# First pair of an attention kernel: other load buffers, its own shift chain for head a's first 12 maxima, and pair 1's preparations inside the first block

## The chip, the cores and the metric

The kernel runs on one core of one Trainium2 chip. The metric is device time in microseconds of one execution. The engines are TensorE (PE, matmuls, with the weight loads counted apart as PEld), VectorE (DVE), ScalarE (ACT), GpSimd (POOL) and SyncE (SP), whose queue issues most DMAs.

## What is computed

Attention over 2 batches of 8 heads, whose queries are pooled two by two, followed by two feed-forward layers:

```python
q_pool = q.reshape(B, H, S // 2, 2, D).mean(axis=3)          # B=2 H=8 S=1152 D=64
scores = np.matmul(q_pool, k.transpose(0, 1, 3, 2)) / np.sqrt(D)
scores = scores - np.max(scores, axis=-1, keepdims=True)
attn = np.exp(scores)
attn = attn / (np.sum(attn, axis=-1, keepdims=True) + 1e-09)
x = np.matmul(attn, v)                                       # to 1152 tokens x 512
h = x @ w_in                                                 # d_ff 2048
g = (a[0] + a[1]*h + a[2]*h*h + a[3]*h*h*h) / (1 + abs(b[0])*abs(h) + abs(b[1])*h*h + 1e-6)
x = g @ w_out
h = x @ w2_in
out = (np.maximum(h, 0) + np.log1p(np.exp(-np.abs(h)))) @ w2_out
```

## The kernel before

All matmuls work on numbers split into a high and a low part of 32 bits, so each product is made from two or three matmuls. The attention runs over eight pairs of heads (a and b of a pair; `j` is the pair, `x` the head), the feed-forward layers follow.

For each pair the kernel first *prepares*: it loads K and Q, adds the queries two by two (`prep_q`, L317 and L318 on POOL), transposes K and Q on PE (`tr_k` L328, `tr_q` L353), casts the high part out of PSUM on ACT (L334, L361), subtracts the low part on DVE (L123 is the subtraction helper, L362), and copies the results by DMA to where each head needs them: `dma_ks` (K's two parts, `KS`), `dma_q` (`QQ`, `QL`), `dma_kh` (a second place of K's high part, `KH`). The buffers `kr`, `qr`, `qs`, `khi`, `klo`, `qhi`, `qlo` and `vr` exist once each. V is split by `prep_v` (L310 on ACT, then a subtraction; for head a on POOL, for head b on DVE).

Then come the *maxima*: 27 fills (`p1_fill`, L397) put 128 pooled queries against 384 keys each into PSUM, and `p1_max` (L402, DVE) takes the largest score of each row. Fill `u` belongs to tile `u // 3`: tiles 0 to 3 are head a, tile 4 is half a and half b and takes four matmuls instead of two, tiles 5 to 8 are head b. The *shift chain* turns the maxima into ten further rows of the query operand: `shift_a` (three small DVE operations, L410, L411, L123), `shift_t` (a matmul, L419), `shift_m` (two DVE products, L426 and L433, into rows 64 to 73 of `QL`). A head's chain waits for 15 maxima.

Then comes the *block* of 36 steps (`s_step`, two matmuls L447 and L448, exponential L451 on ACT). Steps 0 to 17 are head a, in two halves of the queries, steps 18 to 35 head b. Every two steps `s_split` casts the probabilities (L458, ACT) and subtracts (L123, POOL), and `pv` multiplies by V (L470 to L472). PSUM has three tiles `s` (scores, transpositions, shift), three `p1` (maxima) and two for the sums.

The order is written by hand as due times: `A(t, f)` puts function f at step t, where block j starts at step 36 j. `b0`, `b1`, `b2` are the starts of blocks j, j-1 and j-2. A pair is prepared from `b2` on and its maxima are made from `b1` on, so in the steady state pair j+1's maxima and pair j+2's preparations run inside block j. A planner then sorts each engine's queue: what its own model has ready and is due first goes first; within a queue nothing overtakes. `behind(f, ...)` queues f behind the last recorded instruction of the engines named.

The first pair is special. `first_load` (L228) loads K and Q of head a on SP's queue and of head b on ACT's, into `kr` and `qr`. `first_k` and `first_q` transpose each head by itself, with no DMA between. PE runs 24 dummy matmuls at the start (`warm`, L265) and one behind each fill of the first pair. Pair 1's preparations are due beside the first pair's maxima, before block 0 (`k1`, lines "o = b2 + ..."). `constants` and `moe_consts` are queued behind the first pair's splits. Clears and constants stand at the end of the function (L732 to L740).

Of the kernel before, what the change touches and what calls it, by code (L numbers as in the profile page):

```python
# [19 lines left out]
    wu=1,  # L20
# [51 lines left out]
    k1=1,  # L72
# [15 lines left out]
def attn_moe_kernel(tc, q, k, v, w1_in, w1_out, moe_a, moe_b, w2_in, w2_out, out):  # L88
# [140 lines left out]
    def first_load():  # L229
        kr = early.tile([128, C, 2, D], F32, tag="kr", name="kr").rearrange("p c x d -> p (c x d)")  # L230
        kr = kr.rearrange("p (x c d) -> p x c d", x=2, d=D)
        qr = early.tile([128, 2, 5, 2, D], F32, tag="qr", name="qr")
        qs = early.tile([128, 5, 2, D], F32, tag="qs", name="qs")
        for x, eng in enumerate((nc.sync, nc.scalar)):
            eng.dma_start(out=kr[:, x].rearrange("p c d -> p (c d)"),
                          in_=k[0, x].rearrange("(p c) d -> p (c d)", p=128))
            eng.dma_start(
                out=qr[:, x, 0:4].rearrange("p t r d -> p t (r d)"),
                in_=q[0, x, 0:1024].rearrange("(t p r) d -> p t (r d)", p=128, r=2),
            )  # L240
            eng.dma_start(out=qr[0:64, x, 4].rearrange("p r d -> p (r d)"),
                          in_=q[0, x, 1024:S].rearrange("(p r) d -> p (r d)", r=2))
        st["kr", 0], st["qr", 0], st["qs", 0] = kr, qr, qs

    def constants():
        nc.vector.tensor_copy(out=identr, in_=ident)
        nc.vector.tensor_add(out=mask, in0=ident[0:10, 0:5], in1=ident[0:10, 5:10])
        nc.vector.memset(eps, 1e-9)
        for x in range(2):
            nc.gpsimd.memset(KH[x][64:74].bitcast(F32), 1.0)  # L250
# [16 lines left out]
    def first_k(x, g):  # L267
        kr = st["kr", 0]
        t = pps.tile([128, 512], F32, tag="s", name="tk")[0:64, 0:384]
        for i in range(3):  # L270
            nc.tensor.transpose(t[:, i * 128:(i + 1) * 128], kr[:, x, 3 * g + i], ident)
# [103 lines left out]
    def p1_fill(j, u):  # L375
# [4 lines left out]
        if j == 0 and u % 2:  # L380
# [19 lines left out]
    def p1_max(j, u):  # L400
        t, e = divmod(u, 3)
        nc.vector.tensor_reduce(out=st["nm", j][:, t, e:e + 1], in_=st.pop(("p1", j, u)), axis=AX.X,  # L402
                                op=ALU.max, negate=True)

    def shift_a(j, x):
        c = slice(0, 5) if x == 0 else slice(4, 9)
# [3 lines left out]
        nc.vector.tensor_reduce(out=m, in_=nm, axis=AX.X, op=ALU.min)  # L410
# [11 lines left out]
    def shift_m(j, x):  # L422
# [3 lines left out]
        nc.vector.tensor_tensor(  # L426
            out=ql[64:74, c0:c0 + 512].rearrange("p (t i) -> p t i", t=4),
            in0=t[0:10, 0:128].unsqueeze(1).to_broadcast([10, 4, 128]),
            in1=mask[:, m0:m0 + 4].unsqueeze(2).to_broadcast([10, 4, 128]),
            op=ALU.mult,  # L430
        )
        m1, c1, i1 = (4, 512, 0) if x == 0 else (0, 64, 64)
        nc.vector.tensor_scalar(out=ql[64:74, c1:c1 + 64], in0=t[0:10, i1:i1 + 64],  # L433
                                scalar1=mask[:, m1:m1 + 1], scalar2=None, op0=ALU.mult)
# [66 lines left out]
    for j in range(NP):  # L501
# [407 lines left out]
```

## Time and profile before

| | us |
|---|---|
| median of 3 runs (lowest, highest) | 762.19 (761.78, 762.73) |
| the profiled execution | 762.84 |
| its span, first to last instruction | 761.0 |

| engine | busy us | share of the span |
|---|---|---|
| PE | 727.4 | 96% |
| PEld | 680.8 | 89% |
| DVE | 552.6 | 73% |
| ACT | 493.7 | 65% |
| POOL | 294.0 | 39% |

The shares are means over stages with different limits. A matmul's end is modelled, so PE's busy time is no measure of how densely matmuls follow one another; their starts are. "Idle before" in a row is the time in which the engine stood still ahead of that instruction, with what ended it.

### The profile page before, as it was taken

How to read it: one execution, taken by the hardware profiler on the slowest of the kernel's cores; microseconds unless marked ns; L12 is line 12 of the kernel's file. 1: busy time of each engine (PE TensorE's matmuls, PEld its weight loads, DVE VectorE, ACT ScalarE, POOL GpSimd, SP SyncE). 2: the span in 40 equal slices, each digit the busy share in tenths (PEclk: the TensorE clock that was granted, in tenths of full speed). 3: DMA queues.
4: the chain of work that ended last, by engine and by line, in shares of the span. 5: the costliest groups of instructions: out<-in, count | busy, mean ns of one | idle time of the engine just before them, and what ended most of it. 6: DMA issues, size and time to landing. Idle time of an engine off the chain costs nothing.

```text
span 761.0 us, 11752 instructions
## 1 busy us (share of the span) xinstructions
PE 727.4 (96%) x4273; PEld 680.8 (89%) x4273; DVE 552.6 (73%) x885; ACT 493.7 (65%) x921; POOL 294.0 (39%) x233
## 2 busy tenths in 40 slices
PE   8999999999999998888999999999999899999997
PEld 5699999999999997668999999999889779989986
DVE  5777767787777679999999999999987772111122
ACT  3278888888888888986778777866744552222120
POOL 5278796969697877760000000000133432000000
PEclk9999999999999999999999999999999999999999
DMA  4866365646453434332211122221234440001011
GB/s 130 204 154 156 93 159 123 141 114 151 117 114 85 99 99 124 112 115 79 82 58 56 56 84 60 79 70 45 87 105 139 139 139 0 1 1 42 0 42 42
DMA packets 60473, 70.30 MB, mean 92 GB/s; under 512 B 20008, under 2 KB 48512, under 8 KB 60416
## 3 DMA queue, kind: packets, MB, share of 16 engines
q1 hardware_dynamic: 59232, 68.58, 33.4%
q10 hardware_dynamic: 1184, 0.98, 0.4%
q8 instruction: 33, 0.54, 0.3%
q14 instruction: 24, 0.20, 0.1%
HBM read 47.71 MB, written 2.36 MB: 66 GB/s over the span
## 4 chain that ended last, share of the span: by engine, by line
PE 68%; DVE 15%; ACT 8%; issue 3%; DMA 3%; POOL 1%; DVEq 0%; ACTq 0%; POOLq 0%; SPq 0%
PE h L610 18%; PE p L397 10%; PE acc L702 10%; PE acc L660 9%; PE pv L472 4%; PE s L448 4%; PE s L447 4%; PE pv L470 4%; PE pv L471 4%; DMA wraw<-in_moe_w_in_dram 3%; DVE pk L189 3%; DVE pk L183 2%; ACT p L451 2%; ACT ph L458 2%; DVE gl L123 1%
## 5 line engine op out<-in xcount | busy, mean ns | idle before, releaser
L123 POOL TENSOR_TENSOR pl<-p,ph 128x576 fp32r<-128x576 f32 x144 | 209.7, 1471 | 60.9 <-ACT ph L458 40.9
L610 PE MATMUL h<-xh,w 128*128 128x384 f32 x768 | 198.7, 338 | 5.9 <-DVE p L635 5.9
L402 DVE TENSOR_REDUCE nm<-p 128x1 f32<-128x384 f32 x216 | 116.6, 552 | 44.8 <-PE p L397 43.2
L610 PEld LDWEIGHTS h<-xh,w 128*128 128x128 f32 x768 | 140.5, 190 | 8.7 <-issue 6.7
L123 POOL TENSOR_TENSOR w<-pk,w 128x512 fp32r<-128x512 f32 x26 | 39.4, 1517 | 252.4 <-PE h L610 187.6
L451 ACT ACTIVATE p<-s 128x288 f32<-128x288 f32 x288 | 114.5, 408 | 28.2 <-PE s L448 26.8
L610 PE MATMUL h<-xl,w 128*128 128x384 f32 x384 | 129.9, 338 | 0.0
L123 DVE TENSOR_TENSOR gl<-p,gh 128x768 fp32r<-128x768 f32 (+1 forms) x49 | 48.3, 989 | 100.4 <-ACT gh L621 100.3
L472 PE MATMUL pv<-pl,v 128*128 128x288 f32 x288 | 88.3, 307 | 10.8 <-POOL pl L123 10.7
L458 ACT CAST ph<-p 128x576 fp32r<-128x576 f32 x144 | 96.8, 672 | 2.7
L660 PE MATMUL acc<-gh,w 128*128 128x384 f32 x384 | 91.8, 336 | 1.5 <-ACT gh L621 1.5
L702 PE MATMUL acc<-w,gh 128*128 128x512 f32 x288 | 90.3, 394 | 2.2 <-ACT gh L621 1.6
L470 PE MATMUL pv<-ph,v 128*128 128x288 f32 x288 | 86.5, 301 | 0.4 <-ACT ph L458 0.4
L471 PE MATMUL pv<-ph,v 128*64 128x288 f32 x288 | 85.3, 296 | 0.0
L690 ACT ACTIVATE p<-h 128x768 f32<-128x768 f32 (+1 forms) x25 | 19.5, 783 | 90.0 <-PE h L610 90.0
L610 PEld LDWEIGHTS h<-xl,w 128*128 128x128 f32 x384 | 72.8, 190 | 0.0
L660 PEld LDWEIGHTS acc<-gh,w 128*128 128x128 f32 x384 | 68.6, 188 | 2.6 <-ACT gh L621 2.4
L472 PEld LDWEIGHTS pv<-pl,v 128*128 128x128 f32 x288 | 54.6, 190 | 17.9 <-POOL pl L123 17.6
L702 PEld LDWEIGHTS acc<-w,gh 128*128 128x128 f32 x288 | 53.4, 188 | 13.9 <-ACT gh L621 2.4
L189 DVE SCALAR_TENSOR_TENSOR pk<-wraw,pk 128x512 int32<-128x512 int32 x64 | 58.5, 917 | 1.0
L660 PE MATMUL acc<-gl,w 128*128 128x384 f32 x192 | 58.3, 337 | 0.9 <-DVE gl L123 0.9
L702 PE MATMUL acc<-w,gl 128*128 128x512 f32 x144 | 57.1, 396 | 1.5 <-DVE gl L123 1.5
(147 smaller groups left out, 1479.0 us busy)
## 6 DMA issues: line engine op xcount, KB each, us to landing
wraw<-in_moe_w_in_dram SPq DMA_DIRECT2D x32, 512.0 KB, 4.5
wraw<-in_moe_w_out_dram SPq DMA_DIRECT2D x32, 512.0 KB, 3.2
vr<-in_v_dram SPq DMA_DIRECT2D x8, 576.0 KB, 3.7
kr<-in_k_dram SPq DMA_DIRECT2D x15, 288.0 KB, 3.9
qr<-in_q_dram SPq DMA_DIRECT2D x15, 256.0 KB, 3.4
out_dram<-m SPq DMA_DIRECT2D x15, 128.0 KB, 1.7
kha<-ks0a SPq DMA_DIRECT2D x4, 288.0 KB, 3.0
khb<-ks0b SPq DMA_DIRECT2D x4, 288.0 KB, 4.7
```

What stands on the lines that cost most here:

```text
L123: return eng.tensor_tensor(out=o, in0=a, in1=b, op=ALU.subtract)
L189: nc.vector.scalar_tensor_tensor(out=g, in0=raw[:, :, 0], scalar=29, in1=g, op0=ALU.logical_shift_right, op1=ALU.bitwise_or)
L397: m = nc.tensor.matmul(out=o, lhsT=l, rhs=r, start=(a == 0), stop=(a == len(mm) - 1))
L402: nc.vector.tensor_reduce(out=st["nm", j][:, t, e:e + 1], in_=st.pop(("p1", j, u)), axis=AX.X, op=ALU.max, negate=True)
L451: st["last", "exp"] = nc.scalar.activation(out=st["p"][:, s % 2], in_=t, func=AF.Exp).ins
L458: nc.scalar.copy(out=ph, in_=p)
L470: nc.tensor.matmul(out=st["pv", j, g], lhsT=h, rhs=ph, start=(c == 0), stop=False)
L471: nc.tensor.matmul(out=st["pv", j, g][0:64], lhsT=l, rhs=ph, start=False, stop=False)
L472: nc.tensor.matmul(out=st["pv", j, g], lhsT=h, rhs=pl, start=False, stop=(c == C - 1))
L610: nc.tensor.matmul(out=h, lhsT=w[:, wi, wd], rhs=x[:, d, xcols(c)], start=(n == 0), stop=(n == 3 * ND - 1))
L660: nc.tensor.matmul(out=st["acc", c, d], lhsT=w[:, wi, wd], rhs=g, start=(first and n == 0), stop=(last and n == 2))
L702: nc.tensor.matmul(out=st["acc", c, t], lhsT=g[:, t * 128:(t + 1) * 128], rhs=w[:, wi], start=(first and n == 0), stop=(last and n == 2))
```

## The change

It changes only the opening and blocks 0 and 1.

- `first_load` brings K of both heads on SP's queue and Q of both on ACT's, into buffers of the probabilities (tags `p`, `pl`, and `xs0` for the last 64 rows of Q), which leaves `kr` and `qr` to pair 1.
- Constants and clears go to the start of the program; six clears move from POOL to DVE: four of 10 x 640, and two of 10 x 1152 that were part of `constants`. `moe_consts` goes to step 39.
- For the first pair, fills 0 to 11 are followed by a chain of head a's first four tiles (`part=1`), at high priority. Fills 12 to 14 come after it. Fills 15 to 26, the other twelve of head b, are due in steps 0 to 11 of block 0, without dummies behind them. The rest of head a's shift (`part=2`, 64 columns) is due at step 3, head b's chain at step 14.
- Pair 1's preparations move into block 0: query sums due at step -14, key transpositions at 2, 5 and 8, query transpositions at 11 and 14, copies at 11 (K of a), 15 (Q of a), 16 (K of b), 17 (Q of b). Its 27 fills are due one a step from 18 to 44, its chains from 34 and 46. Pair 2's due times stay: loads at 0, query sums at 8, key transpositions at 12, 15 and 18.
- The first pair's second V subtraction goes from DVE to POOL.

```diff
-    k1=1,
+    k1=26,
+    p1s=18,
...
+        rest = late.tile([128, HALF], F32, tag="xs0", name="qrest")[0:64, 0:256]
+        rest = rest.rearrange("p (x r d) -> p x r d", x=2, r=2)
+        kr, qr = [], []
+        for x in range(2):
+            kx = late.tile([128, 2, HALF], F32, tag="p", name="kr0", bufs=4).rearrange("p a b -> p (a b)")
+            qx = late.tile([128, 2, HALF], F32, tag="pl", name="qr0", bufs=5).rearrange("p a b -> p (a b)")[:, 0:512]
+            nc.sync.dma_start(out=kx, in_=k[0, x].rearrange("(p c) d -> p (c d)", p=128))
+            nc.scalar.dma_start(
+                out=qx.rearrange("p (t e) -> p t e", t=4),
                 in_=q[0, x, 0:1024].rearrange("(t p r) d -> p t (r d)", p=128, r=2),
             )
+            nc.scalar.dma_start(out=rest[:, x].rearrange("p r d -> p (r d)"),
+                                in_=q[0, x, 1024:S].rearrange("(p r) d -> p (r d)", r=2))
...
-        (nc.gpsimd if T["qsp"] and x else nc.vector).tensor_add(out=qs[p, c, x], in0=qr[p, x, c, 0], in1=qr[p, x, c, 1])
+        a = qr[x] if g == 0 else st["rest"][:, x].unsqueeze(1)
+        nc.vector.tensor_add(out=qs[p, c, x], in0=a[:, :, 0], in1=a[:, :, 1])
...
-        sub(nc.gpsimd if T["vl"] > x else nc.vector, v2[:, :, 128:192], vr, v2[:, :, 0:64])
+        sub(nc.gpsimd if T["vl"] > x or j == 0 else nc.vector, v2[:, :, 128:192], vr, v2[:, :, 0:64])
...
-        if j == 0 and u % 2:
+        if j == 0 and u < 15 and u % 2:
...
+    def shift_a(j, x, part=0):
+        n = 4 if part == 1 else 5
+        c = slice(0, n) if x == 0 else slice(4, 9)
...
+        if part == 1:
+            nc.vector.memset(m[:, 4:5], 0.0)
+        nc.vector.tensor_reduce(out=m[:, 0:n], in_=nm, axis=AX.X, op=ALU.min)
...
+    def chain(j, x, part):
+        with tc.high_priority():
+            shift_a(j, x, part)
+            shift_t(j, x)
+            shift_m(j, x, part)
...
-                    A(b1 + T["pv"] + T["pvd"] * x, lambda x=x: behind(lambda: prep_v(1, x), "act", "dves"), pr=7)
+                    A(b1 + T["pv"] + T["pvd"] * x, lambda x=x: behind(lambda: prep_v(1, x), "exp", "max"), pr=7)
...
-            A(b1 + T["ft"] + 1, lambda: behind(constants, "dve"))
-            A(b1 + T["ft"] + 1, lambda: behind(moe_consts, "act", "dve"))
+            A(ST + 3, lambda: behind(moe_consts, "sp", "exp", "max"), pr=9)
...
-            A(o + T["pq"], prep_q, j)
+            A((o if j > 1 else b2 + 14) + T["pq"], prep_q, j)
...
-            A(o + T["ks0"], dma_ks, j, 0)
-            A(o + T["q0"], dma_q, j, 0)
-            A(o + T["ks1"], dma_ks, j, 1)
-            A(o + T["q1"], dma_q, j, 1)
+            for x, (tk, tq) in enumerate(((T["ks0"], T["q0"]), (T["ks1"], T["q1"])) if j > 1 else ((21, 25), (26, 27))):
+                A(o + tk, dma_ks, j, x)
+                A(o + tq, dma_q, j, x)
...
-                t0 = b1 + T["p1o"] + u * 4 // 3
+                t0 = -38 + u if u < 12 else -36 + u if u < 15 else u - 15
                 A(t0, p1_fill, j, u, pr=5)
-                A(t0, lambda: behind(lambda: warm(T["wu"]), "pe"), pr=5)
+                if u < 15:
+                    A(t0, lambda: behind(lambda: warm(T["wu"]), "pe"), pr=5)
                 A(t0 + 1, p1_max, j, u, pr=6)
+            A(-25, chain, 0, 0, 1)
+            A(3, chain, 0, 0, 2, pr=7)
+            A(14, chain, 0, 1, 0, pr=7)
         for u in range(27 if j else 0):
-            t0 = b1 + T["p1o"] + u * 4 // 3
+            t0 = b1 + (T["p1o"] + u * 4 // 3 if j > 1 else T["p1s"] + u)
...
-        for x in range(2):
-            t0 = b1 + T["s0"] if x == 0 else b1 + T["s1"]
+        for x in range(2 if j else 0):
+            t0 = b1 + ((T["s0"], T["s1"]) if j > 1 else (T["p1s"] + 16, T["p1s"] + 28))[x]
...
+        nc.vector.memset(zero, 0.0)
         make_identity(nc, ident)
-        nc.vector.memset(zero, 0.0)
...
-                nc.gpsimd.memset(QL[i][x][64:74].bitcast(F32), 0.0)
+                nc.vector.memset(QL[i][x][64:74].bitcast(F32), 0.0)
+        nc.vector.tensor_copy(out=identr, in_=ident)
+        nc.vector.tensor_add(out=mask, in0=ident[0:10, 0:5], in1=ident[0:10, 5:10])
+        nc.vector.memset(eps, 1e-9)
+        for x in range(2):
+            nc.vector.memset(KH[x][64:74].bitcast(F32), 1.0)
```

## Rows read from the trace of the kernel before

**Rows 1.** The page, its first line.
```profile
span 761.0 us, 11752 instructions
```

**Rows 2.** Busy time by stretch: stretch, length, busy us (instructions) of PE, PEld, DVE, ACT, POOL, granted clock, DMA share, GB/s.
```profile
9.18:34.13 24.95, 23.36 (x120) 15.01 (x118) 21.46 (x51) 6.00 (x14) 7.45 (x10) 1.00 0.62 143
34.13:70.92 36.79, 36.57 (x242) 34.80 (x243) 26.35 (x58) 30.17 (x68) 27.80 (x23) 1.00 0.68 159
70.92:107.60 36.68, 36.68 (x258) 36.19 (x257) 27.28 (x56) 31.45 (x72) 30.04 (x25) 1.00 0.53 124
```

**Rows 3.** Timeline of PE, two stretches: start us, duration us, what.
```profile
70.92 0.30 PE L448 MATMUL s<-ql1a,kha 74*128 74x288 f32 x1
71.06 0.34 PE L397 MATMUL p<-ks0a,qq0a 128*128 128x384 f32 x1
71.23 0.34 PE L397 MATMUL p<-ks0a,ql0a 74*128 74x384 f32 x1
71.41 0.29 PE L470 MATMUL pv<-ph,v 128*128 128x288 f32 x1
...
107.60 0.30 PE L448 MATMUL s<-ql0a,kha 74*128 74x288 f32 x1
```

**Rows 4.** Chain of waits: start us, duration us, what.
```profile
45.94 0.33 PE tk L328 x3
```

**Rows 5.** Timeline of all engines, the first 10 us.
```profile
0.97 0.11 DVE L738 MEMSET qq0a<- 128x64 f32 x1
...
1.06 5.33 PE L265 MATMUL wm<-zero 128*64 128x256 bf16 x24 [1.06 <-DVE zero L732]
...
1.48 0.11 DVE L739 MEMSET ql1b<- 64x64 f32 x1
...
4.48 0.62 POOL L740 MEMSET ql0b<- 10x640 f32 x1
...
5.64 0.43 DVE L279 TENSOR_TENSOR qs<-qr 128x256 f32<-128x256 f32 x1 [4.04 <-DMA qr<-in_q_dram]
...
9.08 1.05 POOL L250 MEMSET kha<- 10x1152 f32 x1
```

**Rows 6.** Timeline of DVE, first maxima and constants.
```profile
9.84 0.56 DVE L402 TENSOR_REDUCE nm<-p 128x1 f32<-128x384 f32 x1 [0.25 <-PE p L397]
...
17.63 0.23 DVE L246 CAST identr<-ident 128x128 fp32r<-128x128 f32 x1
...
17.86 1.40 DVE L256 TENSOR_SCALAR a_sb<-a_sb 128x4 f32<-128x4 f32 x1
...
19.71 2.86 DVE L402 TENSOR_REDUCE nm<-p 128x1 f32<-128x384 f32 x6
```

**Rows 7.** Timeline: shift chains of pairs 0 and 2, first shifted scores.
```profile
32.45 0.23 PE L419 MATMUL ts<-identr,s 128*10 128x128 f32 x1
...
33.40 0.68 DVE L426 TENSOR_TENSOR ql0a<-ts,mask 10x512 fp32r<-10x512 f32 x1
...
34.13 0.40 PE L448 MATMUL s<-ql0a,kha 74*128 74x288 f32 x1
...
35.82 0.17 DVE L410 TENSOR_REDUCE m<-nm 128x5 f32<-128x15 f32 x1
...
90.24 1.42 POOL L123 TENSOR_TENSOR pl<-p,ph 128x576 fp32r<-128x576 f32 x1 [0.67 <-ACT ph L458]
90.25 1.44 DVE L123 TENSOR_TENSOR s<-m,s 128x5 fp32r<-128x5 f32 x1
```

**Rows 8.** Groups by line and form, ACT, 34.13 to 70.79 us.
```profile
L334 ACT CAST khi<-tk 128x384 fp32r<-128x384 f32 x3 | 1.4, 471 | 0.1
```

**Rows 9.** Timeline of POOL: the first pair's first probabilities.
```profile
36.65 4.20 POOL L123 TENSOR_TENSOR pl<-p,ph 128x576 fp32r<-128x576 f32 x3 [4.41 <-ACT ph L458]
```

**Rows 10.** Timeline of SP's queue; landing times of the copies into `ks1b`.
```profile
31.14 1.10 SPq L211 DMA_DIRECT2D qq1a<-qhi  x2
...
DMA to landing us min/median/max: 5.9/5.9/5.9
```

More of the change, by code (lines that the diff above doesn't have):

```diff
@@ L229, in first_load @@
     def first_load():
[L230 to L238, printed above, removed]
+        rest = late.tile([128, HALF], F32, tag="xs0", name="qrest")[0:64, 0:256]
[7 more added lines that the diff above has]
+                out=qx.rearrange("p (t e) -> p t e", t=4),
                 in_=q[0, x, 0:1024].rearrange("(t p r) d -> p t (r d)", p=128, r=2),
             )
[L241 to L248, printed above, removed]
-        for x in range(2):
-            nc.gpsimd.memset(KH[x][64:74].bitcast(F32), 1.0)
+            nc.scalar.dma_start(out=rest[:, x].rearrange("p r d -> p (r d)"),
+                                in_=q[0, x, 1024:S].rearrange("(p r) d -> p (r d)", r=2))
+            kr.append(kx.rearrange("p (c d) -> p c d", d=D))
+            qr.append(qx.rearrange("p (t r d) -> p t r d", t=4, r=2))
+        st["qs", 0] = early.tile([128, 5, 2, D], F32, tag="qs", name="qs")
+        st["kr", 0], st["qr", 0], st["rest"] = kr, qr, rest
     def moe_consts():
@@ L401, in p1_max @@
         t, e = divmod(u, 3)
[L402 to L406, printed above, removed]
+        st["last", "max"] = nc.vector.tensor_reduce(
+            out=st["nm", j][:, t, e:e + 1], in_=st.pop(("p1", j, u)), axis=AX.X, op=ALU.max, negate=True).ins
+    def shift_a(j, x, part=0):
+        n = 4 if part == 1 else 5
+        c = slice(0, n) if x == 0 else slice(4, 9)
         nm = st["nm", j][:, c]
@@ L420, in shift_t, with shift_m @@
         st["ts"] = t
-    def shift_m(j, x):
+    def shift_m(j, x, part=0):
         t = st.pop("ts")
@@ L425, in shift_m @@
         m0, c0 = (0, 0) if x == 0 else (1, 128)
[L426 to L431, printed above, removed]
-        m1, c1, i1 = (4, 512, 0) if x == 0 else (0, 64, 64)
-        nc.vector.tensor_scalar(out=ql[64:74, c1:c1 + 64], in0=t[0:10, i1:i1 + 64],
-                                scalar1=mask[:, m1:m1 + 1], scalar2=None, op0=ALU.mult)
+        if part != 2:
+            nc.vector.tensor_tensor(
+                out=ql[64:74, c0:c0 + 512].rearrange("p (t i) -> p t i", t=4),
+                in0=t[0:10, 0:128].unsqueeze(1).to_broadcast([10, 4, 128]),
+                in1=mask[:, m0:m0 + 4].unsqueeze(2).to_broadcast([10, 4, 128]),
+                op=ALU.mult,
+            )
+        m1, c1, i1 = (4, 512, 0) if x == 0 else (0, 64, 64)
+        if part != 1:
+            nc.vector.tensor_scalar(out=ql[64:74, c1:c1 + 64], in0=t[0:10, i1:i1 + 64],
+                                    scalar1=mask[:, m1:m1 + 1], scalar2=None, op0=ALU.mult)
+    def chain(j, x, part):
[3 more added lines that the diff above has]
+            shift_m(j, x, part)
     def qcols(x, half):
@@ L542, in attn_moe_kernel @@
             for u in range(27):
-                t0 = b1 + T["p1o"] + u * 4 // 3
+                t0 = -38 + u if u < 12 else -36 + u if u < 15 else u - 15
                 A(t0, p1_fill, j, u, pr=5)
-                A(t0, lambda: behind(lambda: warm(T["wu"]), "pe"), pr=5)
+                if u < 15:
+                    A(t0, lambda: behind(lambda: warm(T["wu"]), "pe"), pr=5)
                 A(t0 + 1, p1_max, j, u, pr=6)
+            A(-25, chain, 0, 0, 1)
+            A(3, chain, 0, 0, 2, pr=7)
+            A(14, chain, 0, 1, 0, pr=7)
         for u in range(27 if j else 0):
-            t0 = b1 + T["p1o"] + u * 4 // 3
+            t0 = b1 + (T["p1o"] + u * 4 // 3 if j > 1 else T["p1s"] + u)
             A(t0, p1_fill, j, u, pr=T["prf"])
             A(t0 + T["p1m"], p1_max, j, u, pr=T["prm"])
-        for x in range(2):
-            t0 = b1 + T["s0"] if x == 0 else b1 + T["s1"]
+        for x in range(2 if j else 0):
+            t0 = b1 + ((T["s0"], T["s1"]) if j > 1 else (T["p1s"] + 16, T["p1s"] + 28))[x]
+            d = (8, 8) if j > 1 else (1, 4)
             A(t0, shift_a, j, x)
-            A(t0 + T[f"st{x}"], shift_t, j, x, pr=1)
-            A(t0 + T[f"st{x}"] + T["sm"], shift_m, j, x, pr=2)
+            A(t0 + d[x], shift_t, j, x, pr=1)
+            A(t0 + d[x] + T["sm"], shift_m, j, x, pr=2)
         for s in range(ST):
@@ L730, in attn_moe_kernel @@
     if True:
+        nc.vector.memset(zero, 0.0)
         make_identity(nc, ident)
-        nc.vector.memset(zero, 0.0)
         for i in range(2):
             nc.gpsimd.memset(V2[i][:, :, :, 64:128].bitcast(F32), -1.0)
-        for x in range(2):
-            z = slice(576, 640) if x == 0 else slice(0, 64)
-            for i in range(2):
+        for i in range(2):
+            for x in range(2):
+                z = slice(576, 640) if x == 0 else slice(0, 64)
                 nc.vector.memset(QQ[i][x][:, z].bitcast(F32), 0.0)
                 nc.vector.memset(QL[i][x][0:64, z].bitcast(F32), 0.0)
-                nc.gpsimd.memset(QL[i][x][64:74].bitcast(F32), 0.0)
+                nc.vector.memset(QL[i][x][64:74].bitcast(F32), 0.0)
+        nc.vector.tensor_copy(out=identr, in_=ident)
+        nc.vector.tensor_add(out=mask, in0=ident[0:10, 0:5], in1=ident[0:10, 5:10])
+        nc.vector.memset(eps, 1e-9)
+        for x in range(2):
+            nc.vector.memset(KH[x][64:74].bitcast(F32), 1.0)
         ev.sort(key=lambda e: e[:3])
```

3 lines of the change are left out of this document (1 added, 2 removed).

## The prediction

> **What bounds the kernel now.** I read the span and its stretches first. The span is 761.0 us in an execution of 762.84 us; 1.84 us lie around it, and the median of the runs, 762.19 us, is 0.65 us below that execution [rows 1]. I then cut the attention's start by its own marks: 9.18 us (first matmul of the maxima) to 34.13 (first scores that use a shift), and from there two blocks of 36 steps [rows 2]. The reader should see that the blocks are full: 36.68 us for the second block, TensorE (PE) busy in all of it, its matmuls at a pitch that leaves nothing between them. The opening is not full. Its 60 matmuls of 384 columns are worth 60 x 0.175 = 10.5 us at the pitch of the blocks [rows 3], and its transpositions and the shift about 4 us more (some nine groups like that of [rows 4], and single ones); 24.95 us pass. About 10 us of PE time are lost there, although the busy column says 23.36: it counts matmuls whose ends are modelled, and the dummies. VectorE (DVE) is busy for 21.46 of the 24.95 us, so the opening is bound by DVE: 27 maxima, the splits of the first pair, the constants. That is the only stretch in which this change can gain.
>
> **The start.** Loading the first pair into other buffers brings K on SP's queue and Q on ACT's side by side, and frees the old buffers for pair 1, whose loads no longer wait. The borrowed buffers cost nothing: the transpositions have read them before there are probabilities. The change of queues gains nothing by itself: PE runs its 24 dummies from 1.06 to 6.39 us, and DVE adds the queries from 5.64 on, so data that land earlier find DVE occupied. What occupies it is the other half of the edit. DVE is free at about 1.57 us (eight clears of 64 columns start 0.073 us apart) [rows 5]. To it come four clears of 640 columns and two of 1152, 4864 columns. GpSimd (POOL) needs 4 x 0.62 + 2 x 1.05 = 4.58 us for them, which is one bound; 76 times 0.073 = 5.5 us is the other. I take 5.0, and 0.4 us for the three constants now ahead (the first of them 0.23 [rows 6]). DVE then begins with the queries at 1.57 + 5.0 + 0.4 = 7.0 us rather than 5.64, 1.3 us late. Not all of it reaches the first maximum (9.84 us): in these 4.2 us DVE waits for transpositions that PE can now do meanwhile. I take **+0.8 us**, bounds 0 and 1.8.
>
> **The twelfth maximum.** The six maxima from 19.71 us take 2.86 us, 0.477 each; the twelfth is the fifth of these and ends at 22.1 us. The constants and the expert parameters sat in one stretch ahead, 17.63 to 19.26 us, and leave it: -1.6 us. The splits of head b stay where they are, ahead of most of the maxima. So the twelfth ends at 22.1 - 1.6 + 0.8 = 21.3 us.
>
> **The shift chain.** Now only these twelve are waited for, and the chain goes ahead of other DVE work. Three small operations of 0.17 us, then a matmul of 0.23, then a product of 0.68 [rows 7]; with some 0.1 us for each of five hand-overs 1.9 us. Against it stands a row: a subtraction of five columns took 1.44 us when POOL's 1.42 us subtraction had started just before it [rows 7]. In the new order POOL holds, at 18 to 23 us, both subtractions of V for the first pair (the second came from DVE) and the sums of queries for pair 1, right where the chain falls. The Trainium skill (SBUF — State Buffer, Who interferes with whom) says that a DVE instruction with two SBUF inputs contends with a GpSimd instruction that reads SBUF, and this row agrees; one hold of 1.42 us by that rule gives 759.1 us in all, no contention 757.7. I take +1.1 us for the hold, bounds 0 and 2.8 (two holds). Chain: 3.0 us. First shifted scores at 21.3 + 3.0 = 24.3 us, against 34.13: **-9.8 us**.
>
> **What moves behind it.** PE's work isn't removed. Twelve fills of head b (two matmuls of 0.175 us each) go into block 0: 4.2 us. Pair 1's five groups of transpositions go there too: 5 x 0.33 = 1.65 us [rows 4]. As the blocks are PE-bound this comes back in full: **+5.85 us**. Nine of pair 1's fills slide on into block 1; that shifts work between blocks and adds none. ACT gets three casts of 0.47 us and two query casts more in block 0 [rows 8]: 30.17 of 36.79 us busy before, some 32.5 of 38 or more after, no bound on average. The tile 4 fills (u 12 to 14) fit into PE's idle time while the chain runs. The removed twelve dummies lay in idle time and are worth nothing. The expert parameters move to step 39, where DVE is busy for 27.28 of 36.68 us; their 1.6 us hide there. The second V subtraction on POOL: its cover is that POOL has no probabilities until the first pair of steps is done (36.65 us before, its wait before that 4.41 us) [rows 9]; if that cover fails, 1.42 us.
>
> **The start of block 0.** Before, PE had no fills in the first steps, as pair 1's keys were still under way. Now it has those of head b at once. I take **-0.5 us**, bounds 0 and -1.5.
>
> **Copies that become late.** Pair 1's query transpositions are due at step 14 and its fills from step 18. Between them lie three query copies of 0.55 us on SP's queue and a landing of up to 5.9 us [rows 10]; 14.7 + 1.7 + 5.9 = 22.3 steps at worst. SP is also held: pair 2's loads, due at step 0, wait in front for pair 1's key transpositions of step 8. Steps without fills leave PE 0.66 us of work each, and a fill that comes before its copy holds the scores and values queued behind it on PE. I take **+1.1 us**, bounds 0 and 4.
>
> **The sum:** -9.8 + 5.85 - 0.5 + 1.1 = -3.35 us. Against the profiled execution 762.84 - 3.35 = 759.5; against the median **758.8 us**. All best ends: -7.35 us, 754.8. All worst: +2.75 us, 764.9.
>
> **Rivals.**
> 1. *The single key buffer holds ACT (slower).* Pair 2's key transpositions are due at step 12, their casts at 13, into the one buffer that pair 1's copies read until they land. The second head's copies are due at step 16, behind three query copies: 14.7 + 1.7 + 0.5 + 5.9 = 22.8 steps. A cast at its place 13 waits 9.8 us with the exponentials queued behind it, and the transposed tile holds one of three PSUM slots of the scores. That is 758.8 - 1.1 + 9.8 = 767.5 us; it decides once the wait is over 4.5 us. For it: before, these copies were due 13 steps ahead of that cast. Against: the planner puts an instruction into its queue when its model has it ready, and the cast would be put later. Chance 0.15.
> 2. *Block 0 pays it back.* Fills come late and in a heap, block 0 runs at ACT's pace in the hole; the term of 1.1 becomes 4: 761.7 us. Chance 0.16.
> 3. *The chain doesn't get ahead:* the order still has most of head b's maxima in front of the first scores. Then only the constants (-1.6) and the late start (+0.8) remain: 761.4 us. Chance 0.03.
> 4. *PE's clock falls.* The 24 dummies took 0.222 us each, which for 256 columns is the 1.2 GHz level; the granted clock reads 1.00 in all stretches, and the 0.175 us for 384 columns is the 2.4 GHz level [rows 2, 3, 5]. A fall, with a run at the lower level as long as these dummies, costs 5.33 / 2 = 2.7 us: 761.5 us. The Trainium skill (TensorE: Matmul & The Clock Gate, Part 1) says that the clock drops after the array has idled; here it rose before the first transpositions and the trace shows no fall in the opening. Chance 0.03.
>
> **How the numbers follow.** The forecast with its better end has 0.63: all faster. Rivals 2, 3 and 4 lie within 0.2% (1.5 us, about what a measurement of this kernel can tell from no change): 0.22. Rival 1 is slower: 0.15. The range takes the forecast's bounds but for their last half microsecond below, and rival 2 and the near part of rival 1 above: 755.3 to 763.6.
>
> **What would show it.** The first scores with a shift at 23 to 25.5 us; the twelfth maximum at 20.5 to 22; DVE's first sum of queries at 6.5 to 7.5; the first scores of pair 2 (107.60 us before [rows 3]) at 102.5 to 106, and the same lead at the end. Steps right but blocks longer than 38.5 and 39.5 us: rival 2. An exponential that waits behind a key cast: rival 1. What would make the prediction wrong is an order on PE or ACT in which a late copy stands in front.

## The result, and the profile after

The changed kernel takes 772.71 us (median of four runs, 772.30 to 773.08) against 762.14 us for the kernel before in the same runs: a ratio of 1.0137, 95% interval 1.0125 to 1.0150. It is 10.6 us slower, where 758.8 us, 3.4 us faster, was forecast; the range ended at 763.6.

The page of the changed kernel: its first line, PE's line, and the granted clock in the 40 slices of the span (answering [rows 1]).

```profile
span 771.0 us, 11735 instructions
...
PE 732.4 (95%) x4262; PEld 685.4 (89%) x4262; DVE 553.8 (72%) x894; ACT 493.8 (64%) x921; POOL 290.9 (38%) x228
...
PEclk7989999999999999898999999999999999999999
```

Busy time by stretch, with the columns of [rows 2]: first the opening (first fill to first shifted scores), block 0 and block 1, which answer its three rows one for one, then four stretches of 5 us.

```profile
11.23:30.71 19.48, 18.86 (x79) 12.12 (x77) 13.76 (x31) 3.85 (x8) 5.45 (x7) 0.78 0.38 100
30.71:77.66 46.95, 42.15 (x257) 37.65 (x257) 27.57 (x62) 32.77 (x74) 28.14 (x22) 0.93 0.56 123
77.66:117.94 40.28, 40.10 (x272) 39.29 (x273) 32.90 (x70) 31.46 (x71) 31.71 (x28) 1.00 0.54 131
...
10.00:15.00 5.00, 4.58 (x14) 2.94 (x14) 3.32 (x8) 0.81 (x3) 0.35 (x2) 0.50 0.81 167
15.00:20.00 5.00, 5.00 (x20) 3.12 (x18) 2.81 (x5) 1.06 (x2) 0.61 (x1) 0.52 0.00 0
...
45.00:50.00 5.00, 2.87 (x20) 2.35 (x20) 1.58 (x4) 1.31 (x4) 3.17 (x4) 1.00 0.67 150
50.00:55.00 5.00, 3.46 (x13) 2.84 (x14) 0.00 (x0) 3.08 (x7) 4.15 (x3) 0.55 0.75 155
```

Three marks carry the comparison. First shifted scores: 30.71 us, where 24.3 was forecast (34.13 before). Block 0: 46.95 us; by the forecast's terms blocks 0 and 1 together were to take 73.47 + 6.45 = 79.9 us, and they take 87.23, although block 1 with its 40.28 is no surprise. Pair 2's first scores: 117.94 us against 107.60, so 10.3 us late, and the span is 10.0 us longer. So the loss against the forecast, 13.7 us at that mark, has two places: 6.4 us ahead of block 0, and 7.3 us inside it. In both the granted clock reads 0.50 to 0.55 for some 5 to 10 us, at or near the 1.2 GHz level, where it read 1.00 in all three stretches before [rows 2].

The start, from the timeline of the changed kernel (start us, duration us, what, idle time ahead and its releaser):

```profile
1.08 5.26 PE L262 MATMUL wm<-zero 128*64 128x256 bf16 x24 [1.08 <-DVE zero L743]
...
1.34 0.59 DVE L752 MEMSET ql0a<- 10x640 f32 x1 [0.17 <-issue]
...
5.32 1.02 DVE L757 MEMSET kha<- 10x1152 f32 x1 [0.30 <-issue]
...
7.58 0.42 DVE L277 TENSOR_TENSOR qs<-qr 128x256 f32<-128x256 f32 x1
...
8.15 0.60 PE L282 MATMUL tq<-ident,qs 128*64 128x128 f32 x4 [1.81 <-DVE qs L277]
```

From 1.34 to 7.55 us DVE works through the clears (four like the first shown, two like the second, 4.40 us), with small ones between them, and stands still for 0.17 to 0.30 us ahead of each, 1.17 us in all. Its first sum of queries starts at 7.58 rather than 5.64 us [rows 5]. The reader should see the last row: PE ends its dummies at 6.34 us and stands still for 1.81 us, until the sum is there. Then, from about 9.5 to 19.6 us, the granted clock is 0.50.

The shift chain of head a's first twelve maxima (answering [rows 7]):

```profile
26.79 0.15 DVE L411 TENSOR_REDUCE m<-nm 128x4 f32<-128x12 f32 x1
...
27.45 0.56 DVE L400 TENSOR_REDUCE nm<-p 128x1 f32<-128x384 f32 x1 [0.50 <-PE p L395]
...
27.93 0.16 DVE L412 CAST s<-m 128x5 fp32r<-128x5 f32 x1
...
27.99 0.55 DVE L400 TENSOR_REDUCE nm<-p 128x1 f32<-128x384 f32 x1
...
28.46 0.15 DVE L124 TENSOR_TENSOR s<-m,s 128x5 fp32r<-128x5 f32 x1
28.53 1.01 DVE L400 TENSOR_REDUCE nm<-p 128x1 f32<-128x384 f32 x2
...
28.88 0.22 PE L420 MATMUL ts<-identr,s 128*10 128x128 f32 x1
...
29.57 0.68 DVE L428 TENSOR_TENSOR ql0a<-ts,mask 10x512 fp32r<-10x512 f32 x1
...
30.71 0.30 PE L457 MATMUL s<-ql0a,kha 74*128 74x288 f32 x1
```

The chain takes 3.92 us. Four maxima of 0.5 to 0.56 us stand between its operations in DVE's order, and the first of them waits 0.50 us for its fill; the chain waits behind them.

Block 0, where PE loses most of its time:

```profile
43.34 0.52 PE L326 MATMUL tk<-ident,kr 128*128 128x128 f32 x3 [0.77 <-DMA kr<-in_k_dram]
...
44.11 0.29 PE L457 MATMUL s<-ql0a,kha 74*128 74x288 f32 x1
...
45.33 1.42 POOL L315 TENSOR_TENSOR qs<-qr 128x256 f32<-128x256 f32 x2 [2.35 <-PE tq L351]
...
47.12 1.39 POOL L124 TENSOR_TENSOR pl<-p,ph 128x576 fp32r<-128x576 f32 x1
...
48.56 0.40 PE L481 MATMUL pv<-pl,v 128*128 128x288 f32 x1 [2.13 <-POOL pl L124]
...
49.06 0.30 PE L457 MATMUL s<-ql0a,kha 74*128 74x288 f32 x1
...
49.40 0.41 ACT L460 ACTIVATE p<-s 128x288 f32<-128x288 f32 x1 [3.69 <-PE s L457]
...
57.46 1.49 DVE L400 TENSOR_REDUCE nm<-p 128x1 f32<-128x384 f32 x3 [10.22 <-PE p L395]
58.86 1.48 DVE L124 TENSOR_TENSOR klo<-tk,khi 128x384 fp32r<-128x384 f32 x3
```

Pair 2's first transposed keys (`tk`, 43.34 us) wait for their raw keys, with all that stands behind them in PE's queue. Between 44.11 and 49.06 us PE runs no shifted score; POOL's sum of pair 2's queries waits for pair 1's transposition, the low parts of the probabilities stand behind that sum, the values behind these (2.13 us), the scores behind the values, and the exponentials behind the scores (3.69 us). No fill of pair 1 runs before 54.87 us. The three tiles of pair 2's transposed keys are subtracted from only at 58.86 us, three in a row; in the kernel before they came one by one, at 47.20, 50.68 and 54.10 us.

### The profile page after: what moved, and what is told of

The parts are those of the page before. It is cut to its first block, busy times and chain, and to the rows that moved or that the text cites. A ratio compares the mean times of both kernels' runs of the same rounds, so it can differ in the third digit from the quotient of the medians.

```text
span 771.0 us, 11735 instructions
## 1 busy us (share of the span) xinstructions
PE 732.4 (95%) x4262; PEld 685.4 (89%) x4262; DVE 553.8 (72%) x894; ACT 493.8 (64%) x921; POOL 290.9 (38%) x228
## 4 chain that ended last, share of the span: by engine, by line
PE 64%; DVE 19%; ACT 7%; issue 4%; DMA 3%; POOL 1%; DVEq 0%; SPq 0%; ACTq 0%; POOLq 0%
PE h L622 17%; PE acc L714 10%; PE p L395 10%; PE acc L672 9%; PE pv L481 4%; PE s L456 4%; PE s L457 4%; PE pv L479 3%; PE pv L480 3%; DVE pk L190 3%; DMA wraw<-in_moe_w_in_dram 3%; DVE pk L184 2%; ACT p L460 2%; DVE w L124 2%; ACT ph L467 1%
## 5 line engine op out<-in xcount | busy, mean ns | idle before, releaser
L479 PEld LDWEIGHTS pv<-ph,v 128*128 128x128 f32 x288 | 55.9, 194 | 2.9 <-issue 1.7
```

The source lines that it names most:

```text
L479: nc.tensor.matmul(out=st["pv", j, g], lhsT=h, rhs=ph, start=(c == 0), stop=False)
```

## The experiments

Theory A in the expectations is that the six clears on DVE cost the first of the two losses: they delay the first sum, PE stands still, and the clock falls. For the second loss each expectation says its own theories. Each kernel was timed beside the kernel before, and the ratio is to that.

**The clears back on POOL** (everything else as changed):

```diff
-            nc.vector.memset(QL[i][x][64:74].bitcast(F32), 0.0)
+            nc.gpsimd.memset(QL[i][x][64:74].bitcast(F32), 0.0)
-            nc.vector.memset(KH[x][64:74].bitcast(F32), 1.0)
+            nc.gpsimd.memset(KH[x][64:74].bitcast(F32), 1.0)
```

> The changed kernel with its six clears (four of 10x640, two of 10x1152) back on POOL. Theory A (the clears hold DVE to 7.58 us, PE stands idle between 6.34 and 8.15 us, its clock falls and reads 0.50 from 10 to 19.6 us): the first query sum starts near 5.7 us, the granted clock reads 1.00 from 10 to 20 us, the first shifted scores come at 25 to 26.5 us instead of 30.71, block 0 keeps its 47 us; 767 to 768.5 us. Rival B (the opening is bound by the planner's order, not by the clears): first shifted scores after 29 us, 771 us or more.

Measured: 767.04 us, ratio 1.0064 (1.0045 to 1.0084), 5.7 us less than the changed kernel. The first shifted scores come at 24.54 us. The first sum of queries, PE's first transpositions and its first fill; then opening (from the second fill on), blocks 0 and 1 by stretch, and the worst 5 us of block 0:

```profile
4.97 0.43 DVE L277 TENSOR_TENSOR qs<-qr 128x256 f32<-128x256 f32 x1 [3.34 <-DMA qr<-in_q_dram]
...
5.57 0.63 PE L282 MATMUL tq<-ident,qs 128*64 128x128 f32 x4
...
8.45 0.42 PE L395 MATMUL p<-ks0a,qq0a 128*128 128x384 f32 x1
...
9.21:24.54 15.33, 14.68 (x75) 9.72 (x75) 13.17 (x30) 3.17 (x7) 5.46 (x7) 1.00 0.69 158
24.54:69.88 45.34, 41.27 (x258) 36.83 (x257) 27.56 (x62) 32.86 (x74) 28.20 (x22) 0.96 0.59 127
69.88:110.11 40.23, 40.03 (x273) 39.25 (x273) 32.91 (x70) 31.48 (x71) 31.72 (x28) 1.00 0.55 131
...
40.00:45.00 5.00, 3.03 (x12) 2.65 (x13) 0.69 (x2) 1.79 (x4) 2.75 (x4) 0.72 0.95 208
```

The opening has the full clock and ends near the time that the forecast gave, though that forecast had counted 0.8 us for the clears. Its start is earlier than in the kernel before: the first sum follows its load at 4.97 rather than 5.64 us [rows 5], and the first fill is at 8.45 rather than 9.20 us (8.37 to 8.87 us in the ten kernels here with the clears on POOL). So the new load queues do gain some 0.3 to 0.8 us, which the clears on DVE hide. Block 0 is still 45.34 us: the second loss is there without the clears, 5.7 us over the forecast at pair 2's first scores (110.11 us) rather than 7.3. There this kernel is 2.5 us behind the kernel before and at the end of the span 4.1 (765.1 against 761.0); where the other 1.6 us arise, in the part that the change leaves alone, stays open.

**More dummies** (`warm=40` for `warm=24`, clears left on DVE):

> The changed kernel with 40 dummy matmuls at the start instead of 24, so that PE has work until DVE's late query sum; the clears stay on DVE. Theory A (what costs is the clock, the late sum only its 2 us): granted clock 1.00 from 10 to 20 us, first shifted scores at 27 to 28.5 us, 769 to 770.5 us. Rival B (DVE's lateness itself is the cost): clock 1.00 too, but first shifted scores at 30 us or later, 772 us or more. If the clock still reads 0.50 after 10 us, idle time is not what lowers it.

Measured: 768.79 us, ratio 1.0100 (1.0071 to 1.0128). The dummies, PE's next work, and the opening:

```profile
1.08 6.41 PE L262 MATMUL wm<-zero 128*64 128x256 bf16 x40 [1.08 <-DVE zero L743]
...
8.15 0.60 PE L282 MATMUL tq<-ident,qs 128*64 128x128 f32 x4 [0.66 <-DVE qs L277]
...
11.00:26.86 15.86, 15.21 (x79) 10.11 (x77) 13.70 (x32) 3.75 (x8) 5.45 (x7) 1.00 0.46 122
```

PE's idle time shrinks from 1.81 to 0.66 us, the granted clock stays at 1.00, and the first shifted scores come at 26.86 us. So of the 6.17 us between 24.54 and 30.71 the clock is worth 30.71 - 26.86 = 3.85, and DVE's lateness 26.86 - 24.54 = 2.32 us. Time and first scores lie just below what was expected (769 and 27 us).

**Only the clears moved, in the kernel before** (the four clears of `QL` and the two of `KH` to DVE, at the start):

> The kernel before with only the six clears moved from POOL to DVE, at the start of the program. Theory A (late sum, idle PE, fallen clock): the granted clock falls to about 0.5 after 10 us, first shifted scores 4 to 6 us later than 34.13 us, 766 to 768.5 us. Rival B (only the lateness of the first sum counts, since this opening is bound by DVE): clock 1.00, 1.5 to 2 us later, 763.5 to 764.2 us.

Measured: 766.68 us, ratio 1.0060 (1.0042 to 1.0077), 4.8 us slower than the kernel before. PE's first transposition after the dummies, and the stretch after it:

```profile
7.91 0.60 PE L282 MATMUL tq<-ident,qs 128*64 128x128 f32 x4 [1.53 <-DVE qs L277]
...
10.00:15.00 5.00, 4.66 (x14) 2.46 (x14) 3.51 (x8) 0.69 (x2) 0.23 (x1) 0.52 0.28 59
```

The same fall, without the rest of the change. Theory A stands, by three runs: 24 dummies with the sum right behind them (the kernel before, and the clears on POOL) keep 1.00, 24 dummies with 1.53 or 1.81 us of idle time behind them do not, and more dummies in that gap restore it. What the runs do not separate is the idle time from what follows it: from the end of the dummies to the first fill, with only transpositions between, it is 4.6 and 4.9 us in the two kernels with a fall, 2.8 to 3.5 in the three without.

**A second buffer for the sums of queries** (`bufs=2` for the tile `qs`, in the changed kernel), to take away POOL's wait of 2.35 us:

> The changed kernel with two buffers for the summed queries qs, so that POOL's sums for pair 2 need not wait for pair 1's last query transposition. Theory A (that wait of 2.35 us on POOL, with the probabilities' subtractions queued behind it, starts the stall of 43 to 57 us and lowers the clock): POOL shows no wait on tq, the clock reads 1.00 from 50 to 57.5 us, block 0 takes 40 to 42 us instead of 46.95, 766.5 to 769 us. Rival B (late loads and copies cause the stall: pair 2's keys at 43.3 us, pair 1's queries): block 0 still takes 45 us or more, 771 us or more.

Measured: 772.88 us, ratio 1.0134 (1.0102 to 1.0167). It tells nothing about that wait: with the buffer free, pair 3's sum moved to the same place of POOL's order and waited 2.45 us there for the same transposition. The next run gives pair 1's sums a tile of their own, so that nothing else can take it.

**Own buffer for pair 1's sums**, clears on POOL:

```diff
-        qs = early.tile([128, 5, 2, D], F32, tag="qs", name="qs")
+        qs = early.tile([128, 5, 2, D], F32, tag="qs1" if j == 1 else "qs", name="qs")
```

> e1_pool with a buffer of its own for pair 1's summed queries, so that no later pair's sum on POOL waits for pair 1's last query transposition (with two buffers that wait only passed to pair 3's sum, which the planner had pulled to the same place). Theory A (POOL's wait of 1.9 us and the three sums of 1.8 us in front of the probabilities' subtractions start the stall): no POOL wait on tq, values never wait over 1 us for pl between 36 and 44 us, block 0 takes 41 to 42.5 us instead of 45.3, 763 to 764.5 us. Rival B (late copies: without fills for PE the steps run at the pace of ACT and POOL): block 0 takes 44 us or more, 766 us or more.

Measured: 769.47 us, ratio 1.0085 (1.0055 to 1.0116), no better than with the clears on POOL alone. POOL's wait is gone, and block 0 still takes 45.4 us (28.37 to 73.81). The wait was a part of the jam, not its cause. On the way the run shows the hold that the forecast had put into the chain:

```profile
20.56 0.15 DVE L411 TENSOR_REDUCE m<-nm 128x4 f32<-128x12 f32 x1
...
21.34 2.77 POOL L124 TENSOR_TENSOR v<-vr,v 128x576 fp32r<-128x576 f32 x2
...
21.69 2.44 DVE L412 CAST s<-m 128x5 fp32r<-128x5 f32 x1
...
24.65 0.69 PE L395 MATMUL p<-ks0b,qq0b 128*128 128x384 f32 x1 [2.20 <-DVE nm L400]
```

With pair 1's sums earlier on POOL, both subtractions of V fall on the chain: a cast of five columns, 0.16 us elsewhere, takes 2.44 us and ends with the second subtraction. PE, busy until 22.4 us, stands still for 2.20 us behind the maxima that wait too, and from 24.65 to 28.37 us its granted clock is 0.50. The chain takes 7.8 us (20.56 to 28.37), hold and low clock together.

**Pair 1's preparations back in the opening** (old due times, `k1=1`; clears on POOL):

> Clears on POOL (as in e1_pool) and pair 1's preparations back at the due times of the kernel before, in the opening; the first chain of twelve maxima, head b's late fills and pair 1's fills one a step stay. Theory A (the stall of block 0 comes from pair 1's preparations inside it): first shifted scores at 25 to 27.5 us, block 0 takes 37 to 40 us instead of 45.3, 758 to 761.5 us. Rival B (block 0 stalls because it starts some 9 us earlier than its copies and pair 2's preparations were laid out for, wherever pair 1's lie): block 0 takes 43 us or more, 764 us or more.

Measured: 763.07 us, ratio 1.0002 (0.9990 to 1.0014). The first shifted scores come later, at 27.21 us, and block 0 takes 39.5 us, both as theory A had them; the time is 1.6 us above its 758 to 761.5. Block 0 is long only with pair 1's preparations in it; the next run shows that pair 2's count as well.

**Pair 2's preparations six steps later**, clears on POOL:

```diff
-            o = b2 + (T["k1"] if j == 1 else 0)
+            o = b2 + (T["k1"] if j == 1 else 6 if j == 2 else 0)
```

> e1_pool with all of pair 2's preparations due six steps later (key transpositions from step 18, query sums at 14). Theory A (what stalls is pair 2's work in the same steps: its keys' load that PE waits for, its sums on POOL): PE's wait on kr is gone, the scores run on through 37 to 42 us, block 0 takes 41 to 43 us, 763 to 765 us. Rival B (pair 1's own copies are late, pair 2 is only in the neighbourhood): 766 us or more.

Measured: 760.28 us, ratio 0.9968 (0.9955 to 0.9982): faster than both kernels, and more than theory A expected. Block 0 takes 39.46 us (24.94 to 64.40), block 1 40.90. So it is two pairs' preparations in the same steps that make block 0 long: moving either away cures it.

**The same with pair 1's own buffer for sums:**

> Both of the last two: own buffer for pair 1's sums, and pair 2's preparations six steps later, with the clears on POOL. Theory A: block 0 takes 39.5 to 41.5 us, no fall of the clock after 10 us, 761 to 763 us. Rival B (pair 1's copies leave PE without fills from step 12 to 20 whatever pair 2 does): block 0 takes 43 us or more, 765 us or more.

Measured: 761.51 us, ratio 0.9992 (0.9969 to 1.0016). Block 0 is as short (39.4 us), but the first shifted scores come at 26.36 us, as the chain meets POOL's subtractions again. The buffer gains nothing with either placing; the intervals of the kernels with and without it overlap.

**The same six steps with the clears left on DVE** (the changed kernel, that one line apart):

> The kernel of after, clears on DVE as it has them, with nothing but pair 2's preparations six steps later. If the late start and block 0's stretch are independent, the later preparations give what they gave with the clears on POOL, 6.8 us: 772.7 - 6.8 = 765.9 us (764.9 to 767), with the first shifted scores still at 30 to 31 us and block 0 near 40 us. If the fall of the clock and the stretch have a common cause, the gain differs by more than 2 us.

Measured: 765.96 us, ratio 1.0038 (1.0024 to 1.0052), where 765.9 was expected. The opening with its low clock, and block 0:

```profile
31.23:70.70 39.47, 38.33 (x255) 35.43 (x254) 26.92 (x59) 32.35 (x73) 28.61 (x22) 1.00 0.64 142
...
10.00:15.00 5.00, 4.58 (x14) 2.94 (x14) 3.32 (x8) 1.02 (x3) 0.35 (x2) 0.50 0.79 156
```

The two losses add up, within the noise of the times. At pair 2's first scores the later preparations are worth 6.4 us here (117.94 against 111.58 us) and 4.8 with the clears on POOL (110.11 against 105.31), so some 1.6 us of block 0's loss may come with the late start.

**What in pair 2's preparations?** Two runs take one half of them each six steps later, clears on POOL. The keys' part (transpositions, casts, copies):

```diff
+            ok = o + (6 if j == 2 else 0)
-                A(o + T["tk"] + T["tkd"] * g, tr_k, j, g, pr=1)
+                A(ok + T["tk"] + T["tkd"] * g, tr_k, j, g, pr=1)
```

(and `ok` likewise for `tr_k_ev` and `dma_ks`)

> The clears on POOL, and of pair 2's preparations only the keys' part (transpositions, casts, copies) six steps later. If the tiles of transposed keys held between pair 1's preparations make the hole (theory D), this has most of what all six steps later gave: 760 to 762.5 us, block 0 at 39.5 to 41.5 us. If the queries' part does it (GpSimd's sums, their transpositions and copies), it stays at 765 to 768 us.

and the queries' part (`prep_q`, `tr_q`, `tr_q_ev`, `dma_q`):

> The other half: the clears on POOL, and of pair 2's preparations only the queries' part (sums on GpSimd, transpositions, copies) six steps later. By theory D 765 to 768 us, block 0 at 44 us or more; if the queries' part makes the hole, 760 to 762.5 us and block 0 at 39.5 to 41.5 us. If both kernels gain about half, the hole comes from the sum of both.

Measured: the keys' part 760.11 us, ratio 0.9954 (0.9937 to 0.9971); the queries' part 767.42 us, ratio 1.0053 (1.0036 to 1.0071). The keys' part does all of it. Blocks 0 and 1 with the keys later, the first of pair 2's transpositions there, and the subtractions from its first two tiles:

```profile
24.49:63.90 39.41, 38.28 (x255) 35.62 (x254) 26.69 (x61) 32.10 (x73) 27.35 (x22) 1.00 0.66 148
63.90:104.40 40.50, 40.41 (x275) 39.56 (x275) 33.90 (x71) 31.81 (x72) 32.27 (x28) 1.00 0.56 130
...
40.26 0.49 PE L326 MATMUL tk<-ident,kr 128*128 128x128 f32 x3
...
48.00 1.01 DVE L124 TENSOR_TENSOR klo<-tk,khi 128x384 fp32r<-128x384 f32 x2
```

This kernel and the one with all of pair 2's preparations later are the best here (their intervals overlap), and it waits for no raw keys. Its first tile of transposed keys is held all the same, from 40.26 to past 48.00 us, and block 0 is short.

**Is it the single buffers of the keys?** The transposed keys hold PSUM tiles that the scores need, until ACT has cast them and DVE has subtracted from them, into buffers that pair 1's copies still read. Three runs, clears on POOL. Own buffer for the low parts (four probability buffers instead of five make room):

```diff
-            st["klo", j] = early.tile([128, S], F32R, tag="klo", name="klo")
+            st["klo", j] = early.tile([128, S], F32R, tag="klo1" if j == 1 else "klo", name="klo")
-        pl = late.tile([128, 2, HALF], F32R, tag="pl", name="pl", bufs=5)
+        pl = late.tile([128, 2, HALF], F32R, tag="pl", name="pl", bufs=4)
```

> The kernel of after with the six clears back on POOL, pair 1's low key parts in a buffer of their own, and four buffers instead of five for the probabilities' low parts, to make room. In the run with the clears on POOL alone, pair 2's three transposed key tiles (from 36.73 us) are subtracted from only at 51.07 to 52.55 us, three in a row, after the copies of pair 1's low parts out of the single buffer; until then they hold slots that the scores need, and PE runs no more than one score between 47.7 and 51.9 us. Theory C (this holding makes block 0 long): the subtractions follow their tiles, the hole of scores goes, and block 0 is 40 to 42.5 us rather than 45.3; 762 to 764.5 us in all. Rival (the amount of work in these steps, or the order of pair 1's copies and fills, makes it long): the subtractions may come earlier, but block 0 stays within 1 us of 45.3 and the time at 766 to 768 us. Rival (four buffers are too few): POOL or DVE wait for probabilities' buffers in both blocks, and the time rises above 768 us.

Measured: 765.82 us, ratio 1.0025 (1.0007 to 1.0042). The copies of pair 1's second keys due at step 12 of block 0 instead of 16 (22 and 26 in the expectation, which counts from ten steps earlier), without a new buffer:

> The clears back on POOL, and the key copies of pair 1's second head due at step 22 instead of 26 of the plan, ahead of the query copies. Theory C (pair 2's transposed tiles wait for the single buffer of pair 1's low key parts, which these copies read): the buffer comes free some 4 us earlier, the three subtractions of pair 2 come before 49 us instead of at 51.07, and block 0 is 1 to 4 us shorter than 45.3; 763 to 766 us. Rival (the query copies and the fills behind them decide): the query copies leave 1 to 2 us later, the fills of pair 1 with them, and block 0 is the same or longer; 767 to 769 us.

Measured: 766.45 us, ratio 1.0047 (1.0031 to 1.0062). In both the subtractions now follow their tiles (first at 45.85 and 45.53 us rather than 51.07), and the second hole of scores closes; the first one, of 5.1 to 5.3 us from 37.5 us on, stays, and block 0 takes 46.1 and 44.4 us, the first as its rival has it, the second just short of what theory C asks. Own buffer for the high parts, with that early copy:

> The clears on POOL, pair 1's high key parts in a buffer of their own, four buffers for the probabilities' low parts to make room, and the key copies of pair 1's second head at step 22, so that the low key buffer comes free early too. With the clears on POOL alone, pair 2's first tile of transposed keys is ready at 37.3 us and cast at 45.05; between 37.5 and 45.6 us PE runs one score. Theory D (rival 1 of the prediction in another form: the single key buffer puts this cast far back in ScalarE's order, and its tile holds one of three slots of the scores meanwhile): the cast comes within 2 us of its tile, the hole goes, block 0 is 40 to 42 us rather than 45.3, and the time 761 to 764 us. Rival (order and amount of the other work, the slot is not what the scores lack): the cast comes early, but block 0 stays at 44 us or more; 765 to 768 us.

Measured: 766.38 us, ratio 1.0037 (1.0023 to 1.0050).

```profile
38.03 0.52 PE L326 MATMUL tk<-ident,kr 128*128 128x128 f32 x3 [1.68 <-DMA kr<-in_k_dram]
...
38.59 0.48 ACT L332 CAST khi<-tk 128x384 fp32r<-128x384 f32 x1 [1.70 <-PE tk L326]
...
43.12 0.54 DVE L124 TENSOR_TENSOR klo<-tk,khi 128x384 fp32r<-128x384 f32 x1
...
24.51:71.34 46.83, 42.18 (x257) 38.12 (x257) 27.29 (x62) 32.99 (x74) 28.14 (x22) 0.93 0.57 125
```

The cast now follows its tile at once, and block 0 takes 46.83 us all the same. That the single buffers make block 0 long falls with these runs: pair 2's first scores come at 110.70, 109.70 and 112.00 us, against 110.11 with the clears on POOL alone and 104.43 with the keys later. In the medians the three kernels are some 2 us better (2.9 to 3.5 us above the kernel before, with the clears on POOL alone 5.2, with the keys later 2.9 below), but that difference is not in blocks 0 and 1. What no run here took away is the holding of the slot: with its cast early, the first tile was still subtracted from only at 43.12 us, as DVE had the shift and the values in front, and the hole in the scores stays (38.80 to 43.79 us). The kernel with the keys later holds a tile longer and is not slowed by it.

**What is left, and what stays open.** Holes in the scores are not the loss by themselves. With the keys' part later there is one of 4.88 us (44.02 to 48.90), with pair 1's preparations in the opening one of 6.05 us (36.24 to 42.29), and both blocks are short: PE fills them with pair 1's fills. Where the block is long, PE has no fills in the hole: with the clears on POOL the last fill of the first pair starts at 34.2 us and the first of pair 1 at 47.87, and in 40 to 45 us PE is busy for 3.03 of 5 us. Pair 2's key transpositions at their old step fall into just that stretch. That they need PE's other work to hide behind is my reading of these rows. Which part of them jams it, their wait for raw keys (0.3 to 1.75 us in these kernels), the slot that their tile holds, or the order that the planner makes around them (several groups of values in a row with no score), was not separated, as every edit of the one also changes the others. Nor was the clock's share: over the changed kernel's block 0 it reads 0.93, by which an estimate gives at most 0.07 x 46.95 = 3.3 us, and it reads 1.00 in every block 0 of 39.4 to 39.5 us. There the low clock (50 to 60 us) comes after the waits that begin at 43.34 us, so it can enlarge the loss but did not start it.

## Why the prediction was wrong

**The start** is the first step that failed, by size: +0.8 us, bounds 0 and 1.8. The six clears took 4.40 us, less than its lower bound of 4.58, but the sum left out DVE's standing still ahead of them (1.17 us), and the first sum came 1.9 us later than before, at 7.58 us, where 1.3 and 7.0 were forecast. The reasoning that DVE's waits for transpositions would absorb half of it doesn't hold: the first fill came 2.0 us late (11.23 against 9.20), and at the full clock 2.3 us reach the first shifted scores, counted from the kernel with the clears on POOL. That the change of queues gains nothing holds only because of the clears: without them the first fill comes 0.75 us before its old time.

**Rival 4, the clock,** was given a chance of 0.03 and 2.7 us. It came, and cost 3.85 us. The prediction had all that it needed: dummies until 6.39 us, transpositions that wait for a first sum moved to 7.0 us. It asked only what the trace of before shows ("no fall in the opening"), not what PE does in the gap that the change itself makes. The low level lasted some 10 us, about twice as long as the dummies by which the price was set. The Trainium skill (TensorE: Matmul & The Clock Gate, Part 1) has the low level as the state after idling. The traces agree: a granted clock of 0.50 followed 1.81 and 1.53 us of idle time, and stayed away behind 0.66 us.

**The twelfth maximum and the chain** were nearly right in time once the start is set aside, in part by luck. With the clears on POOL the chain's first operation is at 20.61 us, where 21.3 - 0.8 = 20.5 was forecast; but the first fill there is 0.75 us early, so from it to the chain 12.2 us pass where the forecast has 11.3. The first shifted scores are at 24.54 us against 24.3 - 0.8 = 23.5. The chain takes 3.93 us instead of 3.0, for another reason than the forecast's: it does not go ahead of other DVE work. Four maxima stand between its operations, the first waiting for its fill; POOL does not hold it there. POOL's hold exists, though, and at the size of the upper bound: 2.44 us where the order puts both V subtractions on the chain. The Trainium skill (SBUF — State Buffer, Who interferes with whom) names casts among the operations that can take the ports shared with GpSimd, and this row agrees.

**What moves behind it,** +5.85 us, is borne out as part of a sum. With the keys' part later, blocks 0 and 1 take 39.41 + 40.50 = 79.91 us, and the forecast's terms (+5.85, -0.5, +1.1) make 79.92; no run measures the three apart. There nine of pair 1's fills slid into block 1, as forecast; in the changed kernel, whose block 1 takes 40.28 us, eight.

**Copies that become late,** +1.1 us with bounds 0 and 4, is the step that failed most: blocks 0 and 1 take 7.3 us more than forecast, 5.7 with the clears on POOL. Its picture was right, a stretch of steps without fills in which PE has 0.66 us of work each and anything late holds all behind it. What it left out is that pair 2's key transpositions lie in that stretch, with their own wait for raw keys and with three tiles that scores need. The prediction looked at pair 2's loads only as something that delays pair 1's copies.

**Rival 1** had the place, pair 2's key transpositions, and nearly the time of that loss alone (767.5 forecast, 767.04 measured with the clears on POOL). That the times agree is luck. Its mechanism, the single key buffer, is not the cause: with a buffer of its own the cast followed its tile at once and the block stayed long, and at pair 2's first scores the three kernels without that wait lie between 0.4 us earlier and 1.9 us later than the one with it. Rival 2 had a price of 2.9 us on the same stretch, too little; rival 3 didn't occur.

So the forecast of -3.35 us is that of another kernel: with the clears left on POOL and pair 2's keys six steps later the span is 757.6 us, 3.4 us under that of the kernel before. The agreement is partly luck as well: that kernel has no late start, which was to cost 0.8 us, and a chain that is 0.9 us longer than forecast.

## What to carry to other kernels

When work is moved onto an engine at the very start, follow the engine that it feeds through the new gap: the price is the delay and the clock that the gap lets fall. When one stage's work is moved into another, look for the stretch that now has nothing to cover waits, and for what was already due there; two stages' preparations in one place cost more here than their sum of work, and moving the *other* one a few steps was worth more than mending any single wait. Taking away one wait of a jam shows whether it was the cause: here three waits went, one run after another, and the jam stayed.

## What was not expected of the hardware

An idle time of 1.81 us after 5.26 us of dummies was followed, some 1.4 us after PE had work again, by about 10 us at a granted clock of 0.50, in which PE was busy for 4.58 and 5.00 us of two stretches of 5 us; 0.66 us idle after 6.41 us of dummies was not. In another kernel 2.20 us of idle time behind dense fills was followed at once by a granted clock of 0.50. In block 0 the clock fell likewise, to 0.55, after waits of about 2 us and thin work. A cast of five columns on DVE took 2.44 us beside two subtractions on POOL, and ended with the second of them.
